# Local attention and two feed-forward layers on one core: loads merged, mask matmul cut into four tiles, order of the work re-timed

## The chip, the cores and the metric

The kernel runs on one core of a Trainium2 chip. The metric is the device time of one execution in microseconds (us). Three runs of the kernel before gave 480.46, 482.44 and 484.45 us, so the median is 482.44 us.

## The reference

Attention first, for 2 batches, 8 heads, 576 positions, 64 channels; then two feed-forward layers over 1152 tokens, 512 channels and 2048 hidden units. The weights are held as 64-bit words, q, k and v as 32-bit floats.

```python
# attention: mean over groups of 4 positions, dense; plus a band |i-j| < 4 at full length
out_d = sm_attn(q_d, k_d, v_d); out_up = np.repeat(out_d, 4, axis=2)
scores = np.where(np.abs(pos[:, None] - pos[None, :]) < 4, scale * q @ k.T, -1e9)
x = out_up + softmax(scores) @ v            # then [B*S, H*D]
h = x @ w_in                                # layer 1
P = a[0] + a[1]*h + a[2]*h**2 + a[3]*h**3
Q = 1 + abs(b[0])*abs(h) + abs(b[1])*h**2
x = (P / (Q + 1e-6)) @ w_out
h = x @ w_in2                               # layer 2
out = (h * np.tanh(softplus(h))) @ w_out2
```

## The kernel before, in words

**Attention** is cut into units (`unit`, L629). A unit is one pair of heads and four windows of 64 positions; a window is worked as two halves of 32 queries that each look at 48 keys. The ninth window of a batch, left over in each of the four pairs, makes a "mixed" unit that holds one window from each pair, so there are 16 plain units and 2 mixed ones. A pair of heads is made ready once per batch by `prep` (L548): it loads k (L554, L558), transposes it on TensorE (L546), scales it (L587), sums groups of four keys (L597), loads v for the dense part (`vload`, L605, two transfers of 64 and 8 rows) and sums it on POOL (L615, L619). A unit loads q (L639; four transfers where mixed), loads the values of its windows (L653; four transfers, or eight where mixed), transposes q, and in `pe_b` (L699) puts the mask into PSUM with one matmul (eye2 times mask, L702), adds 32 score matmuls of 48 columns (L709) and 8 or 32 dense ones of 144 columns (L717). Each of these works on a 64 by 32 tile of the array. Softmax runs on DVE, ACT and POOL; the transposes of the weights are L786 and L791; L816 and L826 multiply with the values. The result is split into two halves, xh and xl, for exact products.

**The layers** multiply 128-row blocks three times each (high by high, high by low, low by high): L1144 and L1277 in layer 1, L1458, L1514 and L1279 in layer 2, where L1458 belongs to a seven-product scheme whose sums L1480 adds on DVE (`plus`). **Weights** come in 32 tiles of 1 MB (L983, L988) into two raw buffers and are turned into floats: ACT L1000 and L1007, DVE L1014, then the high half (L1026) and the low half (L1031).

**The order** of all instructions on every engine is written out by a planner (`Plan.run`, L114). It plays the kernel through with a cost in us for each task (`add({"dve": 0.43}, ...)`) and issues, on each engine that is free, the ready task with the lowest priority number whose buffers are free. The program keeps that order: an instruction that waits holds everything behind it on its engine. All loads and stores are issued from SP. Priorities are due times: unit i of the first chunk has PROL + PSTEP*i + UOFF[i], its q load lies LOFF earlier, the k load KOFF earlier, the window values VOFF later, the dense values VROFF later; a weight tile is loaded LLEAD ahead and turned into floats CLEAD ahead of its use plus GOFF. The planner has a model of the transfers: at most QUEUED = 8 are under way, each with an issue time and a moving time (L221 to L226). When TensorE has nothing to do in the plan, it gets a **dummy**, a matmul of zeros (`warm`, L526, 480 columns).

Window values have NVW = 2 buffers, q has 3, raw weights 2. The mask is built at the start: two `affine_select` of POOL make `band` (L452, L455), and `masks` (L459) copies it on DVE, 12 copies in three tasks; `under` (L486) zeroes the lower half of eye2 and mask.

Of the kernel before, what the change touches and what calls it, by code (L numbers as in the profile page):

```python
# [12 lines left out]
BF16 = mybir.dt.bfloat16  # L13
# [4 lines left out]
ALU = mybir.AluOpType  # L18
AX = mybir.AxisListType

NEG = -1.0e9
# [58 lines left out]
class Plan:  # L80
# [33 lines left out]
    def run(self, names):  # L114
# [79 lines left out]
        while True:  # L194
            for e in names:
# [3 lines left out]
                while ready[e]:  # L199
# [73 lines left out]
def kernel(  # L273
# [22 lines left out]
    TW = 384  # L296
# [8 lines left out]


    ident = const.tile([128, 128], F32, name="ident")
    eye2 = const.tile([128, 128], BF16, name="eye2")
    mask = const.tile([128, 11, WK], BF16, name="mask")
    band = const.tile([64, 92], BF16, name="band")  # L310
    blank = const.tile([128, 480], BF16, name="blank")
# [53 lines left out]
    kn_s = lay("att", NKN, 768, parts=96)  # L365
    vr_s = lay("att", 1, 1024, (4, 4, D), parts=72)
    qn_s = lay("att", NQN, 256)
    vw_s = lay("att", NVW, 512, (4, 2, D), parts=64 + WK)
    s_s = lay("att", 2, 256, (4, 64))
    pd_s = lay("att", 2, SD)  # L370
# [78 lines left out]


    def bands():
        nc.gpsimd.affine_select(  # L452
            out=band, in_=band, compare_op=ALU.is_ge, fill=NEG, base=-8, pattern=[[1, 92]], channel_multiplier=-1,
        )
        nc.gpsimd.affine_select(  # L455
            out=band, in_=band, compare_op=ALU.is_ge, fill=NEG, base=14, pattern=[[-1, 92]], channel_multiplier=1,
        )
# [13 lines left out]

    def eyes():
        for h in range(2):
            nc.vector.tensor_copy(out=eye2[:64, 64 * h:64 * h + 64], in_=ident[:64, :64])
# [11 lines left out]
    def under():  # L486
        nc.vector.memset(eye2[64:], 0.0)
        nc.vector.memset(mask[64:], 0.0)

    t_m = add({"dve": 0.1}, lambda: nc.vector.memset(band, 0.0), -1900)  # L490
    t_un = add({"dve": 0.4}, under, -880)
    t_cd = add({"dve": 0.6}, zeros, -1000)
    t_bn = add({"pool": 0.5}, bands, -900, after=[t_m])
    t_mk = [
        add({"dve": 0.2 + 0.05 * len(ws)}, lambda x=(i, ws): [masks(x[0], *w) for w in x[1]], (-890, MKP, MKP)[i], after=[t_bn])
        for i, ws in enumerate((((0, 1), (1, 1), (2, 1), (3, 1)), ((4, 4),), ((8, 4),)))
    ]
    t_bias = add({"pool": 0.1}, biases, -20)
    t_i16 = add({"dve": 0.26}, eyes, -900, after=[t_id])
    t_ab = add({"sp": 0.9}, c_sp, -34, dma=[(0.65, 0.1), (0.5, 0.1)])  # L500
    A0, A1, A2, A3 = (cf[:, i:i + 1] for i in range(4))
    S0, S1 = (cf[:, i:i + 1] for i in range(4, 6))

# [26 lines left out]
    plan.filler = (warm_s + sc_s + pt_s + po_s, ((t_bl, warm),), 0.19)  # L530


    class Unit:
# [14 lines left out]
    def prep(bb, p, prio, slots, start):  # L548
# [62 lines left out]
        m0 = add({"sp": 1.25}, vload, prio + VROFF, take=[vr], chain="vr", dma=[(0.65, 0.8), (0.6, 0.12)])  # L611

        def va(e):
            tv = vr.v
# [14 lines left out]
    def unit(u, slots, start):  # L629
# [4 lines left out]
        qn, vw, qp, qT, qx = Buf(qn_s + xq), Buf(vw_s + xv), Buf(slots["q"]), Buf(qT_s), Buf(qx_s)  # L634
        sc, pt, po, px = Buf(slots["s"]), Buf(slots["pt"]), Buf(slots["po"]), Buf(px_s)
        tm, s, pd, pT, od, xt = Buf(tm_s), Buf(s_s), Buf(pd_s), Buf(pT_s), Buf(od_s), Buf(xt_s)
        mix = [qx] if mixed else []

        def qload():  # L639
            for i, p in enumerate(pairs):  # L640
                w, m = wins[i][1], n // len(pairs)
                src = q[bb, 2 * p:2 * p + 2, 64 * w:64 * w + 2 * m, :]
                nc.sync.dma_start(  # L643
                    out=qn.v[m * i:m * i + m].rearrange("p (r h d) -> p r h d", h=2, d=D),
                    in_=src.rearrange("h (p r) d -> p r h d", r=2),
                )

        l0 = add({"sp": 0.65}, qload, prio - LOFF, take=[qn], chain="ld", dma=[(0.65, 0.24)] * 4 if mixed else [(0.65, 0.58)])

        m0 = MASK0[kind]  # L650
        keys = [(p, [window(kind, w, b) for b in range(2)]) for p, w in wins]

        def vload():  # L653
            for w0, nb in ((0, 4), (2, 4)) if not mixed else [(w, 2) for w in range(4)]:
                p, (k0, k1) = keys[w0]
                for hh in range(2):
                    src = v[bb, 2 * p + hh]
                    nc.sync.dma_start(
                        out=vw.v[64 * (w0 // 2):64 * (w0 // 2) + WK, 2 * (w0 % 2):2 * (w0 % 2) + nb, hh, :],
                        in_=bass.AP(src.tensor, src.offset + k0 * D, [[D, WK], [(k1 - k0) * D, nb], [1, D]]),  # L660
                    )

        vl = add({"sp": 1.0}, vload, prio + VOFF, take=[vw], chain="vw", dma=[(0.45, 0.11)] * 8 if mixed else [(0.45, 0.33)] * 4)

        def pe_a():
            q2 = qp.v[:, :2 * n].rearrange("c (p r) -> c p r", r=2)
            for r in range(2):
                flip(q2[:, :, r], qn.v, r, n)
# [30 lines left out]
        def pe_b():  # L699

            hs = [slice(0, 64), slice(64, 128)]
            nc.tensor.matmul(  # L702
                sc.v[:, :nw * WK], eye2, mask[:, m0:m0 + nw].rearrange("p w x -> p (w x)"), start=True, stop=False,
            )
# [17 lines left out]
        tb = add(  # L722
            {"pe": 1.6 if mixed else 0.86}, pe_b, prio,
            after=tq + [kv_done[p] for p in pairs] + [t_i16, t_un, t_mk[kind]],
            take=[sc, tm, s, pd],
            use=[qT] + mix, chain="pb",
        )
# [81 lines left out]
        def pe_e():  # L809
# [10 lines left out]
            for m in range(2):  # L820
                for b in range(2):
                    for hh in range(2):
                        for a in range(2):
                            h, r = hs[hh ^ a], slice(64 * a, 64 * a + WK)
                            c = 128 * m + h.start + HB * b
                            nc.tensor.matmul(  # L826
                                px.v[h, a, 64 * m + HB * b:64 * m + HB * b + HB], vw.v[r, 2 * m + b, hh ^ a, :],
                                pT.v[r, c:c + HB], start=True, stop=True,
                            )

# [603 lines left out]
    def seven(st):  # L1434
# [42 lines left out]
        def plus(dst, i, src, after, and_=None):  # L1477
# [96 lines left out]
```

## Time and profile before

| what | us |
|---|---|
| median of three runs | 482.44 (480.46 to 484.45) |
| the profiled execution's own time | 482.31 |
| its span, first to last instruction | 480.4 |
| TensorE matmul busy | 469.4 (98%) |
| TensorE weight load busy | 429.1 (89%) |
| DVE busy | 377.0 (78%) |
| ACT busy | 338.3 (70%) |
| POOL busy | 57.1 (12%) |

Around the span lie 1.9 us. A busy time counts overlapping instructions once; matmuls follow one another before the former has ended, so the spacing of their starts, not their duration, is what one costs. The transfer lines count the 16 DMA engines of the core together.

### The profile page before, as it was taken

What the parts mean: (1) busy time and instruction counts of PE and PEld (TensorE: products, weight loads), DVE (VectorE), ACT (ScalarE), POOL (GpSimd) and SP (SyncE); (2) the same over time, 40 slices, a digit from 0 to 9 for tenths busy, and PEclk for the clock granted to TensorE, in tenths of its full rate; (3) what the DMA queues carried; (4) which work ended last, traced back from release to release, by engine and by line L of the source; (5) the groups of instructions that cost most, each with busy time, mean ns of one, the idle gap of its engine ahead of it and who ended that gap; (6) DMA issues with size and microseconds to landing.
All of it is one profiled execution on the core that took longest, in us unless ns stands there. A gap on an engine that the chain in (4) does not pass through costs nothing.

```text
span 480.4 us, 9823 instructions
## 1 busy us (share of the span) xinstructions
PE 469.4 (98%) x4052; PEld 429.1 (89%) x4052; DVE 377.0 (78%) x565; ACT 338.3 (70%) x529; POOL 57.1 (12%) x80
## 2 busy tenths in 40 slices
PE   8998999999999999999999999999999999999996
PEld 4667888889999999999999999898989898989885
DVE  6677999899899968997998999988596669524342
ACT  5678898786889799998879797578666446422320
POOL 2644434563000000000000000000000000000000
PEclk9999999999999999999999999999999999999999
DMA  9878887611522312343022022134304220000103
GB/s 170 196 178 198 243 200 188 166 37 35 176 89 88 123 54 89 96 125 131 0 89 88 1 88 89 39 111 146 143 15 162 87 89 1 1 0 0 67 0 132
DMA packets 45981, 47.18 MB, mean 98 GB/s; under 512 B 30576, under 2 KB 31344, under 8 KB 45936
## 3 DMA queue, kind: packets, MB, share of 16 engines
q1 hardware_dynamic: 45936, 46.54, 33.7%
q8 instruction: 32, 0.52, 0.5%
q14 instruction: 13, 0.11, 0.1%
HBM read 44.17 MB, written 2.36 MB: 97 GB/s over the span
## 4 chain that ended last, share of the span: by engine, by line
PE 73%; DVE 13%; DMA 8%; ACT 3%; SPq 2%; issue 1%; ACTq 0%
PE psum L1279 19%; PE psum L1144 18%; PE psum L1277 15%; PE psum L1458 11%; PE psum L1514 5%; DMA att<-in_q_dram 3%; DMA raw<-in_moe_w_in_dram 3%; DVE wt L1014 1%; PE psum L826 1%; DMA att<-in_v_dram 1%; DVE xl L1300 1%; PE psum L546 1%; SPq L643 1%; DVE wrk L1318 1%; DVE wo L1031 1%
## 5 line engine op out<-in xcount | busy, mean ns | idle before, releaser
L1144 PE MATMUL psum<-xh,wi 128*128 128x384 f32 (+1 forms) x336 | 83.4, 319 | 0.2 <-DVE wrk L1173 0.2
L1277 PE MATMUL psum<-gg,wo 128*128 128x384 f32 (+1 forms) x480 | 76.3, 313 | 0.0
L1277 PEld LDWEIGHTS psum<-gg,wo 128*128 128x128 f32 x480 | 72.8, 189 | 0.4 <-issue 0.2
L1144 PEld LDWEIGHTS psum<-xh,wi 128*128 128x128 f32 x336 | 59.1, 189 | 1.4 <-issue 0.9
L1144 PE MATMUL psum<-xl,wi 128*128 128x384 f32 (+1 forms) x168 | 52.4, 312 | 0.0
L1279 PE MATMUL psum<-wo,gg 128*128 128x512 f32 x216 | 51.7, 391 | 0.0
L1279 PE MATMUL psum<-wo,late_g 128*128 128x512 f32 x216 | 51.3, 391 | 0.0
L1279 PEld LDWEIGHTS psum<-wo,late_g 128*128 128x128 f32 x216 | 40.4, 188 | 8.0
L1279 PEld LDWEIGHTS psum<-wo,gg 128*128 128x128 f32 x216 | 40.4, 188 | 7.9
L1014 DVE SCALAR_TENSOR_TENSOR wt<-wt,raw 128x1024 int32<-128x1024 int32 x32 | 40.0, 1252 | 6.8 <-ACT wt L1000 6.5
L1000 ACT ACTIVATE wt<-raw 128x1024 f32<-128x1024 f32 x32 | 36.5, 1140 | 10.9 <-DVE wo L1031 4.8
L1007 ACT ACTIVATE raw<-raw 128x1024 int32<-128x1024 uint16 x32 | 36.7, 1147 | 5.1 <-DMA raw<-in_moe_w_out_dram 3.4
L1514 PE MATMUL psum<-xh,wi 128*128 128x384 f32 x128 | 34.5, 335 | 0.0
L1144 PEld LDWEIGHTS psum<-xl,wi 128*128 128x128 f32 x168 | 31.8, 189 | 0.0
L1390 DVE TENSOR_TENSOR part<-psum,part 128x512 f32<-128x512 f32 x27 | 17.8, 687 | 13.7 <-PE psum L1279 13.7
L1144 PE MATMUL psum<-xh,late_r 128*128 128x384 f32 x96 | 25.5, 334 | 0.0
L527 PE MATMUL psum<-blank 128*128 128x480 bf16 x86 | 22.9, 390 | 1.2 <-DVE band L490 1.2
L1031 DVE TENSOR_TENSOR wo<-wt,wo 128x1024 fp32r<-128x1024 f32 x14 | 17.1, 1219 | 8.7 <-ACT wo L1026 8.7
L1026 ACT ACTIVATE wo<-wt 128x1024 fp32r<-128x1024 f32 x11 | 11.7, 1062 | 17.1 <-DVE wt L1020 7.7
L1514 PEld LDWEIGHTS psum<-xh,wi 128*128 128x128 f32 x128 | 23.3, 188 | 0.2
L1164 ACT ACTIVATE wrk<-psum 128x768 f32<-128x768 f32 (+1 forms) x27 | 19.8, 734 | 5.1 <-PE psum L1144 4.8
L1088 ACT ACT_TABLE_LOAD x17 | 21.8, 1283 | 0.3
(165 smaller groups left out, 1043.5 us busy)
## 6 DMA issues: line engine op xcount, KB each, us to landing
raw<-in_moe_w_in_dram SPq DMA_DIRECT2D x16, 1024.0 KB, 6.0
raw<-in_moe_w_out_dram SPq DMA_DIRECT2D x16, 1024.0 KB
att<-in_v_dram SPq DMA_DIRECT2D x64, 48.0 KB, 4.0
out_dram<-part SPq DMA_DIRECT2D x9, 256.0 KB, 2.1
att<-in_q_dram SPq DMA_DIRECT2D x16, 128.0 KB, 4.2
att<-in_k_dram SPq DMA_DIRECT2D x6, 288.0 KB, 4.5
att<-in_v_dram SPq DMA_DIRECT2D x6, 256.0 KB, 5.7
wrk<-in_k_dram SPq DMA_DIRECT2D x2, 288.0 KB
```

The costliest lines, as they stand in the source:

```text
L527: nc.tensor.matmul(view[:, :480], blank[:, :128], blank, start=True, stop=True)
L1000: nc.scalar.activation(out=t.v, in_=words(r)[:, :, 1].bitcast(F32), func=AF.Prelu if fold else AF.Identity, scale=2.0 ** -112, **({"alpha" ...
L1007: nc.scalar.activation(out=words(r)[:, :, 0], in_=r.v.bitcast(U16).rearrange("p (n four) -> p n four", four=4)[:, :, 1], func=AF.Copy, sca ...
L1014: nc.vector.scalar_tensor_tensor(out=ti, in0=ti, scalar=3, in1=words(r)[:, :, 0], op0=ALU.logical_shift_left, op1=ALU.bitwise_or)
L1031: ENG[e].tensor_tensor(out=w.v[:, 1], in0=s.v, in1=w.v[:, 0].bitcast(F32), op=ALU.subtract)
L1088: nc.scalar.preload_act_table_set(name)
L1144: nc.tensor.matmul(st.h.v[:, i, :T], w.v[:, ww, ks], xx[:, kk, c0:c0 + T], start=(nn == 0 and (st.big or i == 0)), stop=(nn == 3 * KD - 1 ...
L1164: nc.scalar.activation(out=vw(st.a), in_=H(), func=AF.Square)
L1277: nc.tensor.matmul(A(d)[:, :T], w.v[:, ww, lo + d * 128:lo + (d + 1) * 128], vw(gg)[:, i, :], start=start, stop=stop)
L1279: nc.tensor.matmul(A(d), vw(gg)[:, i, sl], w.v[:, ww, lo:lo + DM], start=start, stop=stop)
L1458: nc.tensor.matmul(dst.v[:, :TW], wv.v[:, ww, at:at + 128], x(h, kk), start=bool(take) and nn == 0, stop=nn == 5, skip_group_check=not take,)
L1514: nc.tensor.matmul(h.v[:, i, :TW], w.v[:, ww, at:at + 128], xx[:, kk, c0:c0 + TW], start=nn == 0, stop=nn == 3 * KD - 1)
```

## The change

It does the following.

- Window values get a third buffer (NVW 3). A mixed unit's values come in four transfers in place of eight; the four windows lie in another order in the buffer.
- A mixed unit's q comes in one transfer in place of four, as 64 positions by 8 heads, and is transposed by four transposes of 64 rows. It takes the place of two of the q buffers.
- The dense values of a pair come in one transfer of 72 rows in place of two of 64 and 8 rows (8 pairs).
- The mask matmul of 128 rows by 128 columns becomes four on tiles of 64 by 32; eye2, mask and band are laid out twice, in the upper and the lower 64 partitions. `under` goes; `masks` makes 24 copies in place of 12, `bands` four `affine_select` in place of two.
- The two loads of a and b move from SP to ACT's queue and to the very start.
- Dummies have 416 columns in place of 480.
- The planner adds 0.8 us of moving time for every 7 us moved (FETCH, for packets that load instructions). The due times change: CLEAD 14 to 20, LLEAD 40 to 30, OLAG 18 to 26, KOFF 9 to 17, and others. `plus` (L1480) gets a priority 15 earlier.

```diff
-LEAD, CLEAD, LLEAD, OLAG = 38, 14, 40, 18
-PROL, PSTEP, VOFF, VROFF, LOFF, KOFF = -45, 2.5, 2, -1, 7, 9
+LEAD, CLEAD, LLEAD, OLAG = 38, 20, 30, 26
+PROL, PSTEP, VOFF, VROFF, LOFF, KOFF = -45, 3.0, -1, 3, 8, 17
-NKN, NVW, NXT, NQN = 2, 2, 3, 3
+NKN, NVW, NXT, NQN = 2, 3, 3, 3
+FETCH = (0.8, 7.0)
-UOFF = [-3.0, 0.0, 0.0, 3.0, 4.5, 3.0, 3.0, -1.5, 6.0, 0.0, 0.0, -4.5, -4.5, 4.5, 6.0, 4.5, -1.5, -1.5]
-GOFF = [0.0, 0.0, 0.0, 0.0, -4.0, -4.0, -10.0, -6.0, 2.0, -4.0, 10.0, 12.0]
+UOFF = [1.5, 6.0, 6.0, 10.5, 13.5, 16.5, 4.5, 21.0, 9.0, 6.0, -6.0, -3.0, 0.0, 7.5, -1.5, 9.0, -7.5, -12.0]
+GOFF = [0.0, 2.0, 0.0, 4.0, -4.0, -4.0, -8.0, -30.0, 28.0, 2.0, -2.0, 22.0]
...
-                            moved = max(moved, end + 0.3) + move
+                            first = max(moved, end + 0.3)
+                            moved = first + move + FETCH[0] * (int((first + move) / FETCH[1]) - int(first / FETCH[1]))
...
-        for b in range(2):
-            h = slice(HB * b, HB * b + HB)
+        for r0 in range(0, 128, HB):
+            b, h = r0 // HB % 2, slice(r0, r0 + HB)
...
-        nc.sync.dma_start(out=a_sb, in_=a.partition_broadcast(128))
-        nc.sync.dma_start(out=b_sb, in_=b.partition_broadcast(128))
+        nc.scalar.dma_start(out=a_sb, in_=a.partition_broadcast(128))
+        nc.scalar.dma_start(out=b_sb, in_=b.partition_broadcast(128))
...
-        nc.tensor.matmul(view[:, :480], blank[:, :128], blank, start=True, stop=True)
+        nc.tensor.matmul(view[:, :416], blank[:, :128], blank, start=True, stop=True)
...
-            for lo, hi in ((0, 64), (64, 72)):
-                nc.sync.dma_start(out=dst[lo:hi], in_=src[lo:hi])
+            nc.sync.dma_start(out=dst, in_=src)
...
+            if mixed:
+                nc.sync.dma_start(out=qn.v, in_=q[bb, :, 64 * w:64 * w + 64].rearrange("h s d -> s h d"))
...
-            for w0, nb in ((0, 4), (2, 4)) if not mixed else [(w, 2) for w in range(4)]:
-                p, (k0, k1) = keys[w0]
-                for hh in range(2):
+            for a in range(2):
+                p, ks = keys[2 * a]
+                for i in range(2):
+                    src = v[bb, 2 * p + (0 if mixed else i)]
+                    k0, far = (ks[i], S) if mixed else (ks[0], ks[1] - ks[0])
...
-            nc.tensor.matmul(
-                sc.v[:, :nw * WK], eye2, mask[:, m0:m0 + nw].rearrange("p w x -> p (w x)"), start=True, stop=False,
-            )
+            for b in range(2):
+                for h in hs:
+                    r0 = h.start + HB * b
+                    nc.tensor.matmul(
+                        sc.v[r0:r0 + HB, :nw * WK], eye2[h, HB * b:HB * b + HB],
+                        mask[h, m0:m0 + nw].rearrange("p w x -> p (w x)"), start=True, stop=False, tile_position=(h.start, r0),
+                    )
...
-            return add({"dve": t_dve(TW)}, fn, pr, after=after, use=[src, dst])
+            return add({"dve": t_dve(TW)}, fn, pr - HP, after=after, use=[src, dst])
```

## Rows read from the trace of the kernel before

**Rows 1.** Busy time of the engines in five stretches (window, its length, engines, clock, DMA).
```profile
0.00:33.00 33.00, 30.01 (x488) 18.46 (x489) 21.81 (x72) 21.22 (x56) 15.98 (x30) 1.00 0.90 194
33.00:48.00 15.00, 13.38 (x276) 11.20 (x278) 11.07 (x34) 12.92 (x32) 6.14 (x10) 1.00 0.71 167
48.00:96.00 48.00, 46.68 (x838) 41.17 (x837) 45.11 (x91) 40.68 (x96) 22.80 (x26) 1.00 0.80 200
96.00:122.50 26.50, 25.95 (x538) 23.33 (x537) 24.52 (x51) 18.33 (x48) 11.66 (x16) 1.00 0.23 53
122.50:475.50 353.00, 352.36 (x1925) 334.36 (x1924) 272.71 (x318) 245.12 (x300) 0.52 (x1) 1.00 0.22 75
```

**Rows 2.** The same stretches, the dummies of L527 alone (PE, PEld, clock, DMA).
```profile
0.00:33.00 33.00, 17.39 (x67) 6.82 (x67) 1.00 0.90 194
33.00:48.00 15.00, 1.07 (x4) 0.29 (x3) 1.00 0.71 167
48.00:96.00 48.00, 4.04 (x15) 1.42 (x15) 1.00 0.80 200
```

**Rows 3.** The chain that ended last, up to 60 us (start, us, what).
```profile
17.15 2.02 SPq L983
19.27 6.06 DMA att<-in_q_dram
...
26.64 6.37 DMA raw<-in_moe_w_in_dram
...
35.94 0.66 SPq L643
36.65 0.61 SPq L643
37.31 0.61 SPq L643
37.96 5.14 DMA att<-in_q_dram
43.10 0.09 issue
43.19 0.41 PE psum L546 x2
```

**Rows 4.** PE timeline: mask matmul, a unit's scores, dummies, first L1144.
```profile
21.62 0.25 PE L702 MATMUL psum<-mask,eye 128*128 128x192 bf16 x1
21.80 0.55 PE L709 MATMUL psum<-att 64*32 64x48 f32 x32
...
29.39 1.78 PE L527 MATMUL psum<-blank 128*128 128x480 bf16 x8
...
32.74 0.38 PE L527 MATMUL psum<-blank 128*128 128x480 bf16 x1
32.78 0.46 PE L1144 MATMUL psum<-xh,wi 128*128 128x256 f32 x1
```

**Rows 5.** The chain again: two transposes of 128 columns, a mixed unit's 32 dense matmuls.
```profile
44.31 0.22 PE psum L786 x2
...
48.43 0.98 PE psum L717 x32
```

**Rows 6.** DMA queue of the first 33 us (packets, MB, share of 16 engines).
```profile
q1 hardware_dynamic: 10508, 6.32, 88.7%
```

**Rows 7.** What SP waited for up to 120 us, then from 92 to 120 us.
```profile
SPq L658 <- PE psum L826: 12.6, 6, 4.7
...
SPq L658 <- PE psum L826: 11.2, 4, 4.7
```

**Rows 8.** SP's timeline: loads of a and b; issues of dense values at the start.
```profile
2.62 1.19 SPq L609 DMA_DIRECT2D att<-in_v_dram  x2
...
27.37 0.49 SPq L481 DMA_DIRECT2D a_sb<-in_moe_a_dram  x1
27.90 0.43 SPq L482 DMA_DIRECT2D b_sb<-in_moe_b_dram  x1
```

**Rows 9.** DVE at the start: mask copies, then the first sum over q.
```profile
2.81 2.35 DVE L464 COPY mask<-band 32x48 bf16<-32x48 bf16 x12
...
6.36 0.42 DVE L683 TENSOR_REDUCE att<-psum 128x64 f32<-128x256 f32 x1 [1.20 <-PE psum L546]
```

**Rows 10.** Waits over the span: ACT for raw weights, PE for window values, for L1480.
```profile
ACT wt L1000 <- DMA raw<-in_moe_w_in_dram: 4.2, 4, 2.3
...
308.25 0.44 PE L1458 MATMUL psum<-xh,late_r 128*128 128x384 f32 x1 [0.64 <-DVE wrk L1480]
```

**Rows 11.** Landing times of the w_in loads (issue to landing, min/median/max).
```profile
DMA to landing us min/median/max: 5.0/6.0/9.4
```

More of the change, by code (lines that the diff above doesn't have):

```diff
@@ L307 @@
     ident = const.tile([128, 128], F32, name="ident")
-    eye2 = const.tile([128, 128], BF16, name="eye2")
+    eye2 = const.tile([128, 64], BF16, name="eye2")
     mask = const.tile([128, 11, WK], BF16, name="mask")
-    band = const.tile([64, 92], BF16, name="band")
-    blank = const.tile([128, 480], BF16, name="blank")
+    band = const.tile([128, 92], BF16, name="band")
+    blank = const.tile([128, 416], BF16, name="blank")
     a_sb = const.tile([128, 4], F32, name="a_sb")
@@ L367 @@
     qn_s = lay("att", NQN, 256)
+    qm_s = [Place("att", qn_s[-2].lo, 512, (8, D), 64)]
     vw_s = lay("att", NVW, 512, (4, 2, D), parts=64 + WK)
@@ L451, in bands @@
     def bands():
-        nc.gpsimd.affine_select(
-            out=band, in_=band, compare_op=ALU.is_ge, fill=NEG, base=-8, pattern=[[1, 92]], channel_multiplier=-1,
-        )
-        nc.gpsimd.affine_select(
-            out=band, in_=band, compare_op=ALU.is_ge, fill=NEG, base=14, pattern=[[-1, 92]], channel_multiplier=1,
-        )
+        for h in (slice(0, 64), slice(64, 128)):
+            nc.gpsimd.affine_select(
+                out=band[h], in_=band[h], compare_op=ALU.is_ge, fill=NEG, base=-8, pattern=[[1, 92]], channel_multiplier=-1,
+            )
+            nc.gpsimd.affine_select(
+                out=band[h], in_=band[h], compare_op=ALU.is_ge, fill=NEG, base=14, pattern=[[-1, 92]], channel_multiplier=1,
+            )
     def masks(kind, w, n):
-        for b in range(2):
-            h = slice(HB * b, HB * b + HB)
+        for r0 in range(0, 128, HB):
+            b, h = r0 // HB % 2, slice(r0, r0 + HB)
             lo = window(kind, w, b) - 64 * w + 11
@@ L473, in eyes @@
         for h in range(2):
-            nc.vector.tensor_copy(out=eye2[:64, 64 * h:64 * h + 64], in_=ident[:64, :64])
+            nc.vector.tensor_copy(out=eye2[64 * h:64 * h + 64], in_=ident[64 * h:64 * h + 64, 64 * h:64 * h + 64])
     def biases():
@@ L480, in c_sp @@
     def c_sp():
-        nc.sync.dma_start(out=a_sb, in_=a.partition_broadcast(128))
-        nc.sync.dma_start(out=b_sb, in_=b.partition_broadcast(128))
+        nc.scalar.dma_start(out=a_sb, in_=a.partition_broadcast(128))
+        nc.scalar.dma_start(out=b_sb, in_=b.partition_broadcast(128))
     add({"act": 1.3}, lambda: nc.scalar.preload_act_table_set("natural_log_exp_and_others"), -1000)
     t_id = add({"pool": 1.1}, lambda: make_identity(nc, ident), -1000)
-    def under():
-        nc.vector.memset(eye2[64:], 0.0)
-        nc.vector.memset(mask[64:], 0.0)
     t_m = add({"dve": 0.1}, lambda: nc.vector.memset(band, 0.0), -1900)
-    t_un = add({"dve": 0.4}, under, -880)
     t_cd = add({"dve": 0.6}, zeros, -1000)
-    t_bn = add({"pool": 0.5}, bands, -900, after=[t_m])
+    t_bn = add({"pool": 1.0}, bands, -900, after=[t_m])
     t_mk = [
-        add({"dve": 0.2 + 0.05 * len(ws)}, lambda x=(i, ws): [masks(x[0], *w) for w in x[1]], (-890, MKP, MKP)[i], after=[t_bn])
+        add({"dve": 0.4 + 0.1 * len(ws)}, lambda x=(i, ws): [masks(x[0], *w) for w in x[1]], (-890, MKP, MKP)[i], after=[t_bn])
         for i, ws in enumerate((((0, 1), (1, 1), (2, 1), (3, 1)), ((4, 4),), ((8, 4),)))
@@ L499 @@
     t_i16 = add({"dve": 0.26}, eyes, -900, after=[t_id])
-    t_ab = add({"sp": 0.9}, c_sp, -34, dma=[(0.65, 0.1), (0.5, 0.1)])
+    t_ab = add({"act": 1.15}, c_sp, -2000, dma=[(0.65, 0.1), (0.5, 0.1)])
     A0, A1, A2, A3 = (cf[:, i:i + 1] for i in range(4))
@@ L607, in vload @@
             dst = vr.v.rearrange("p (h t) f d -> p h (t f d)", h=2)
-            for lo, hi in ((0, 64), (64, 72)):
-                nc.sync.dma_start(out=dst[lo:hi], in_=src[lo:hi])
-        m0 = add({"sp": 1.25}, vload, prio + VROFF, take=[vr], chain="vr", dma=[(0.65, 0.8), (0.6, 0.12)])
+            nc.sync.dma_start(out=dst, in_=src)
+        m0 = add({"sp": 0.65}, vload, prio + VROFF, take=[vr], chain="vr", dma=[(0.65, 1.0)])
         def va(e):
@@ L633, in unit @@
         xq, xv = (wide_s["qn"], wide_s["vw"]) if start else ([], [])
-        qn, vw, qp, qT, qx = Buf(qn_s + xq), Buf(vw_s + xv), Buf(slots["q"]), Buf(qT_s), Buf(qx_s)
+        qn, vw, qp, qT, qx = Buf(qm_s if mixed else qn_s + xq), Buf(vw_s + xv), Buf(slots["q"]), Buf(qT_s), Buf(qx_s)
         sc, pt, po, px = Buf(slots["s"]), Buf(slots["pt"]), Buf(slots["po"]), Buf(px_s)
@@ L639, in qload @@
         def qload():
-            for i, p in enumerate(pairs):
-                w, m = wins[i][1], n // len(pairs)
-                src = q[bb, 2 * p:2 * p + 2, 64 * w:64 * w + 2 * m, :]
+            w = wins[0][1]
+            if mixed:
+                nc.sync.dma_start(out=qn.v, in_=q[bb, :, 64 * w:64 * w + 64].rearrange("h s d -> s h d"))
+            else:
                 nc.sync.dma_start(
-                    out=qn.v[m * i:m * i + m].rearrange("p (r h d) -> p r h d", h=2, d=D),
-                    in_=src.rearrange("h (p r) d -> p r h d", r=2),
+                    out=qn.v.rearrange("p (r h d) -> p r h d", h=2, d=D),
+                    in_=q[bb, 2 * pairs[0]:2 * pairs[0] + 2, 64 * w:64 * w + 2 * n].rearrange("h (p r) d -> p r h d", r=2),
                 )
-        l0 = add({"sp": 0.65}, qload, prio - LOFF, take=[qn], chain="ld", dma=[(0.65, 0.24)] * 4 if mixed else [(0.65, 0.58)])
+        l0 = add({"sp": 0.65}, qload, prio - LOFF, take=[qn], chain="ld", dma=[(0.45 if mixed else 0.65, 0.58)])
         m0 = MASK0[kind]
@@ L653, in vload @@
         def vload():
-            for w0, nb in ((0, 4), (2, 4)) if not mixed else [(w, 2) for w in range(4)]:
-                p, (k0, k1) = keys[w0]
-                for hh in range(2):
-                    src = v[bb, 2 * p + hh]
+            for a in range(2):
[3 more added lines that the diff above has]
+                    k0, far = (ks[i], S) if mixed else (ks[0], ks[1] - ks[0])
+                    here = vw.v[64 * a:64 * a + WK]
                     nc.sync.dma_start(
-                        out=vw.v[64 * (w0 // 2):64 * (w0 // 2) + WK, 2 * (w0 % 2):2 * (w0 % 2) + nb, hh, :],
-                        in_=bass.AP(src.tensor, src.offset + k0 * D, [[D, WK], [(k1 - k0) * D, nb], [1, D]]),
+                        out=here[:, 2 * i:2 * i + 2].rearrange("k w h d -> k (w h) d") if mixed else here[:, :, i],
+                        in_=bass.AP(src.tensor, src.offset + k0 * D, [[D, WK], [far * D, 4], [1, D]]),
                     )
-        vl = add({"sp": 1.0}, vload, prio + VOFF, take=[vw], chain="vw", dma=[(0.45, 0.11)] * 8 if mixed else [(0.45, 0.33)] * 4)
+        vl = add({"sp": 1.0}, vload, prio + VOFF, take=[vw], chain="vw", dma=[(0.45, 0.33)] * 4)
         def pe_a():
+            if mixed:
+                for i in range(nw):
+                    nc.tensor.transpose(
+                        qp.v[:, 64 * i:64 * i + 64], qn.v[:, 2 * i:2 * i + 2].rearrange("s h d -> s (h d)"), ident[:64, :64],
+                    )
+                return
             q2 = qp.v[:, :2 * n].rearrange("c (p r) -> c p r", r=2)
@@ L722, in unit @@
         tb = add(
-            {"pe": 1.6 if mixed else 0.86}, pe_b, prio,
-            after=tq + [kv_done[p] for p in pairs] + [t_i16, t_un, t_mk[kind]],
+            {"pe": 1.52 if mixed else 0.78}, pe_b, prio,
+            after=tq + [kv_done[p] for p in pairs] + [t_i16, t_mk[kind]],
             take=[sc, tm, s, pd],
@@ L826, in pe_e @@
                             nc.tensor.matmul(
-                                px.v[h, a, 64 * m + HB * b:64 * m + HB * b + HB], vw.v[r, 2 * m + b, hh ^ a, :],
+                                px.v[h, a, 64 * m + HB * b:64 * m + HB * b + HB], vw.v[r, 2 * b + m if mixed else 2 * m + b, hh ^ a, :],
                                 pT.v[r, c:c + HB], start=True, stop=True,
```

4 lines of the change are left out of this document (2 added, 2 removed).

## The prediction

> **What bounds the kernel now.** I read the busy times by stretch first. From 122.5 to 475.5 us TensorE is busy for 352.36 of 353 us, at a granted clock of 1.00 (2.4 GHz) [rows 1]: this part is matmul work that the change doesn't touch, and it can't shrink. What can shrink is time in which TensorE waits, and that lies ahead of 122.5 us in two forms: idle time, and dummies. Dummies show as busy, so the second view counts them [rows 2]. Eight of them in a row take 1.78 us with the last one's tail of 0.38, so one costs (1.78 - 0.38) / 7 = 0.20 us [rows 4], and the loss is:
>
> - 0 to 33 us: 67 x 0.20 = 13.4 us of dummies and 33 - 30.01 = 3.0 us idle, 16.4 us;
> - 33 to 48: 4 x 0.20 + 1.6 = 2.4 us;
> - 48 to 96: 15 x 0.20 + 1.3 = 4.3 us;
> - 96 to 122.5: 0.55 us, with no dummy; after that 0.64 us at one place [rows 10].
>
> So 24.3 us are lost in all and every gain comes out of these. The cut at 33 us is where the first hidden-layer matmul starts, 32.78 us [rows 4]. The third view, the chain that ended last, says what the waits are: up to 48 us it runs through SP's issues and the landings of q and of the first weights, 5 to 6.4 us each [rows 3]. The DMA engines are 0.90 busy up to 33 us, 0.71 in the next stretch, 0.80 up to 96 us and 0.23 after it [rows 1]. The early part is bound by transfers and their order, the late part by TensorE.
>
> **The change part by part.** The sum goes against the profiled execution, 482.31 us, which is within 0.15 us of the median, so the same figure serves for both.
>
> *Mixed q in one transfer.* On the chain, three issues of 0.66, 0.61 and 0.61 us precede the last of the four q transfers, whose landing takes 5.14 us and lets TensorE go on at 43.2 us [rows 3]. One issue in their place takes 1.9 us out of the chain. The loss of that stretch is 2.4 us, so all of it can be had: -1.9 us. The bytes stay the same. If the k load and the values behind it come later instead, the gain is 0; if the q moves ahead of the weight load before it as well, it is the whole 2.4. The second mixed unit's q and values come at the end of attention, where TensorE has no dummies: nothing there.
>
> *Dense values in one transfer, a and b from ACT.* Two issues take 1.19 us [rows 8], so four pairs up to 33 us free 4 x 0.6 = 2.4 us of SP, and a and b free 0.49 + 0.43 = 0.9 us. But the queue's own share is 88.7% of 33 us [rows 6], so only 3.7 us of the stretch are free for transfers to move into, and the first landing takes its part of these. Of the 3.3 us I count 1.3. The loads of a and b then stand ahead of the table load on ACT, which has nothing else to do up to the first landing; cost nothing. If the cover is gone, 0.9 us.
>
> *Due times in the first 33 us.* 6.32 MB move there [rows 6]; the first chunk needs 4 pairs and 4 units: by the shapes 4 x (0.29 k + 0.13 q + 0.29 v + 0.19 window values) + one weight tile of 1.05 MB = 4.7 MB. The other 1.6 MB, at 194 GB/s 8.2 us, come early for what follows. Loading k 8 us earlier and weights 10 us later in due time can bring the needed part forward, but what is put off is due directly afterwards. I take -1.5 us, from 0 to -8.2; with the issues that is -2.8 us of 16.4.
>
> *Third buffer for window values, four transfers for eight.* SP waits 12.6 us for L826 to give such a buffer back, which looks like the prize. But 11.2 us of these lie from 92 us on [rows 7], where TensorE is busy for 25.95 of 26.5 us [rows 1]. Only 1.4 us stand in the hungry part. The mixed unit saves four issues as well. From 48 to 96 us, where 4.3 us are lost, I take a third, -1.4 us; the ends are 0 and -4.3. After 96 us -0.3 us.
>
> *Mask in four tiles.* Now the mask matmul starts 0.18 us before the first score matmul [rows 4]. A tile needs 192 columns, by the dummies' 0.20 us for 480 columns 0.08 us. Four at once make 0.08, one after the other 0.32 us. The trace has the same tiles: a mixed unit's 32 dense matmuls of 144 columns take 0.98 us, while two f32 transposes of 128 columns take 0.22 us [rows 5]. So a matmul of 144 columns alone would need 0.12 us and 32 of them 4.0 us: four run at once. I take 0.08, 18 x -0.10 = -1.8 us of TensorE work. Where TensorE waits for loads this only makes room for a dummy: half the units stand past 48 us, -0.9 us. The ends are -1.8 and 18 x 0.14 = +2.5 us.
> The Trainium skill speaks against this: its page "TensorEngine Tiling (Array Packing)", section "Restrictions and Gotchas", says that different row tiles can't use one PSUM bank at the same time. All four mask tiles write one bank from two row halves, so two rounds would be needed, 0.16 us, and the gain would be 18 x -0.02 = -0.4 us. The trace's dense matmuls write one bank from both row halves and don't bear this out.
>
> *Mask copies.* 12 copies take 2.35 us on DVE up to 5.16 us, and then DVE stands 1.2 us until q has been transposed [rows 9]. Twelve more, at 0.196 us, end some 2.0 us later (the memsets that go give back 0.4), so the first sum over q comes 0.8 us late; k's sums stand behind it. The first landing sets that stretch, and dummies follow; I count +0.4, ends 0 and +0.8.
>
> *Dummies of 416 columns.* A dummy ends 0.03 us earlier where real work becomes ready in its course; with some 20 groups of dummies and half of that each -0.3 us, ends 0 and -0.6. If the shorter ones lost the granted 1.00, each us at 1.2 GHz would cost half a us; no stretch ahead of 475.5 us shows that [rows 1].
>
> *`plus` earlier.* The 0.64 us [rows 10] go if DVE gets to L1480 in time: -0.5 us, ends 0 and -0.64, since what is passed is not needed sooner. The chance that a later DVE step then waits is left in the range.
>
> Sum: -1.9 - 2.8 - 1.4 - 0.3 - 0.9 + 0.4 - 0.3 - 0.5 = -7.7 us. These are not independent: the first three want the same free DMA time, and DVE is 45.1 of 48 us busy from 48 us and 24.5 of 26.5 us after it [rows 1], so what TensorE does earlier must find DVE earlier, too. I strike a fifth: -6.2 us, **476.1 us**. The likeliest case's own range is 473 to 479 us.
>
> **The rivals.**
>
> *Transfers were hidden anyway.* The queue is full up to 33 us, what is loaded earlier displaces something else, and the third buffer works where TensorE is busy. For it: 0.90 busy DMA, and rows 7. Against it: 0.71 in the next stretch. Then the mixed q's half, the mask and `plus` stay: -1.0 - 0.9 - 0.5 + 0.4 = -2.0, 480.3 us.
>
> *The weights come late (slower).* The planned time from a weight load to its turning falls from 40 - 14 = 26 to 30 - 20 = 10 us of due time. A w_in load takes 5.0 to 9.4 us to land [rows 11]. The point from which this decides is a landing 10 us after the load's due time: then L1000 waits on ACT, and the softmax steps queued behind it, and DVE behind these. Now ACT loses 4.2 us in 4 such waits, 1.05 each [rows 10]. Eight tiles are loaded up to 96 us; if every one waited as long, and half of the gain stayed, 482.3 + 8 x 1.05 - 3.1 = 487.6 us. Against it: half of the landings take 6.0 us or less, and none 10.
>
> *Dense values on fewer DMA engines.* 72 rows don't divide by sixteen; if they go to twelve engines with six rows each, that is more than the five rows of the busiest engine now, where 64 and 8 rows are spread. By the stretch's mean, 33 x 0.887 / 6.32 = 4.6 us a MB [rows 6], 0.288 MB take 1.33 us spread evenly at 4.5 rows; five rows are 1.48 us, six 1.78. Four such loads up to 33 us and four after it, 0.3 us each, cost 2.4 us if nothing else fills the free engines: 478.5 us.
> The Trainium skill has the rule of this case on "DMA: Bandwidth & Descriptors", section "Why a DMA increments its semaphore by 16 and not by 1": a transfer uses the largest number of engines up to 16 that divides its slowest dimension, for 72 that is 12. The trace's rows add up all engines, so no row shows it yet.
>
> *More than I count.* With the order right, the put-off 8.2 us and the 4.3 us become reachable to a good half: about -11 us, 471 us.
>
> **How the numbers follow.** Forecast 0.46, more than that 0.13, transfers hidden 0.20, fewer engines 0.10, weights late 0.11. A measurement of this kernel tells about 1% from no change, 4.8 us: faster is below 477.6, slower above 487.3 (the three runs differ by 4). The forecast is below 477.6 in four fifths of its cases, 0.37, the greater gain always, fewer engines in a third, 0.03, hidden in 0.02: 0.55. Weights late is above 487.3 in somewhat over half, and a tail from broken order elsewhere brings it to 0.09. The rest, 0.36, is same. The range goes from 470 (greater gain) to 483 (hidden, with the mask's dear end), leaving out the late weights.
>
> **What would show it.** Right: fewer than 67 dummies up to the first L1144 and that start before 31 us; no idle time of some 1.6 us behind the first mixed q, and one q issue there; L702's four tiles 0.08 to 0.1 us ahead of L709; SP's wait for L826 gone without a change of TensorE after 96 us; the dense stretch of layer 2 as long as before. Wrong: dummies as many as before (hidden), ACT waits for raw weights of over 2 us in number (late), landings of the dense values longer than now (fewer engines).

## The result and the profile after

The changed kernel takes 484.63 us (median of 17 runs, 483.48 to 487.61) where the kernel before took 481.62 in as many runs on the same chips. The ratio is 1.006 (95% interval 1.0044 to 1.0076): slower by 0.6%, where 476.1 us and a gain of over 1% were forecast. The profiled execution took 484.25 us, its span 482.5. A few executions in this document ran in a slower state of the chip; they count in the medians and not in the ratios.

The same five stretches of the changed kernel, all engines (to be read against [rows 1]):

```profile
0.00:33.00 33.00, 30.00 (x477) 19.26 (x478) 22.09 (x86) 19.96 (x57) 14.45 (x31) 1.00 0.90 196
33.00:48.00 15.00, 15.00 (x282) 11.69 (x281) 10.84 (x24) 11.59 (x26) 7.94 (x10) 1.00 0.55 138
48.00:96.00 48.00, 48.00 (x841) 41.85 (x840) 45.32 (x90) 40.53 (x93) 21.79 (x23) 1.00 0.76 198
96.00:122.50 26.50, 26.50 (x577) 24.00 (x577) 25.97 (x56) 19.73 (x54) 13.96 (x18) 1.00 0.21 49
122.50:475.50 353.00, 352.31 (x1983) 334.57 (x1982) 273.98 (x321) 246.06 (x302) 0.78 (x1) 1.00 0.23 77
```

And its dummies alone (L526 now; against [rows 2]):

```profile
0.00:33.00 33.00, 18.66 (x83) 8.27 (x83) 1.00 0.90 196
33.00:48.00 15.00, 5.80 (x28) 2.40 (x27) 1.00 0.55 138
48.00:96.00 48.00, 6.12 (x28) 2.49 (x28) 1.00 0.76 198
```

From 33 to 122.5 us TensorE is never idle, and it does less for it: 56 dummies stand there where 19 stood, 139 in all against 86. Ten in a row (at 20.20 us) take 1.92 us with the last one's tail of 0.34, so one costs (1.92 - 0.34) / 9 = 0.175 us. The loss, counted as in the prediction, is 83 x 0.175 + 3.0 = 17.5 us up to 33 us (16.4 before), 4.9 us up to 48 (2.4), 4.9 up to 96 (4.3), none up to 122.5 (0.55), and 0.7 after it: 28.0 us against 24.3. If the 18 mask matmuls each give back the 0.09 us shown below, that is 1.6 us, and 3.7 - 1.6 = 2.1 us is the difference of the spans. The sum is rough, since the tail of the matmul ahead of a gap counts as busy, and the 1.6 us were not shown by themselves. But it says what has to be explained: where the waits, now dummies, come from.

The chain that ended last, by engine, before and after:

```profile
PE 73%; DVE 13%; DMA 8%; ACT 3%; SPq 2%; issue 1%; ACTq 0%
```

```profile
PE 85%; DVE 11%; ACT 3%; issue 1%; ACTq 0%
```

Transfers and SP's issues made 10% of it and are gone. In their place stands TensorE's own order, the dummies in it.

The loads don't all come earlier. The third w_in tile is issued at 32.82 us for 35.49, but the first mixed q at 46.60 us for 35.94. The first w_in tile is issued when it was before (17.14 us) and must have landed by about 24.5 us, as no w_in load takes longer than 6.9 us; yet ACT, whose order now has the softmax of two units ahead of it, turns it into floats 5 us later. ACT before, then ACT and the first hidden-layer matmul of the changed kernel:

```profile
24.36 1.12 ACT L1000 ACTIVATE wt<-raw 128x1024 f32<-128x1024 f32 x1 [0.44 <-DMA raw<-in_moe_w_in_dram]
```

```profile
29.37 1.14 ACT L1011 ACTIVATE wt<-raw 128x1024 f32<-128x1024 f32 x1
...
36.21 0.43 PE L1155 MATMUL psum<-xh,wi 128*128 128x256 f32 x1
```

That matmul started at 32.78 us before [rows 4]. What SP waited for in the changed kernel, for a buffer of window values (L659) and for the first mixed q (L640):

```profile
SPq L659 <- PE psum L837: 12.4, 10, 3.0
...
SPq L640 <- PE psum L545: 3.3, 1, 3.3
```

The first is as long as before, 12.6 us [rows 7], with three buffers in place of two. The second is new: the mixed q lies over two of the plain q buffers, and SP holds back all that stands behind it until the transposes (L545) have read these.

Two places of the start, first TensorE and then DVE of the changed kernel (against [rows 4, 9]); the column after the time is the duration:

```profile
9.43 0.55 PE L720 MATMUL psum<-att 64*32 64x48 f32 x32 [0.89 <-ACT att L682]
...
13.11 0.26 PE L712 MATMUL psum<-mask,eye 64*32 64x192 bf16 x4
13.20 0.51 PE L720 MATMUL psum<-att 64*32 64x48 f32 x32
```

```profile
6.02 1.32 DVE L468 COPY mask<-band 32x192 bf16<-32x192 bf16 x6
7.37 0.16 DVE L513 TENSOR_REDUCE cf<-cf 128x1 f32<-128x4 f32 x1
...
8.40 0.23 DVE L505 TENSOR_SCALAR cf<-a_sb,cf 128x3 f32<-128x3 f32 x1
8.54 0.42 DVE L690 TENSOR_REDUCE att<-psum 128x64 f32<-128x256 f32 x1
```

At 13.11 us the four tiles stand 0.09 us ahead of the scores (0.18 before), and all four take 0.26 us, as long as the one matmul of before with its tail: they run at once. On DVE (the first line has the last six of the 24 mask copies) the first sum over q starts at 8.54 us, 6.36 before. The copies end at 7.34 us, 2.2 us later than before, and the arithmetic on a and b, which had come at 34 us before, takes the next 1.2 us. The first unit's scores start at 9.43 us, where the kernel before had them at 8.25.

The mixed q (L640) is one transfer now, and TensorE goes on to its transposes (L669) without a gap:

```profile
46.60 0.63 SPq L640 DMA_DIRECT2D att<-in_q_dram  x1
```

```profile
51.47 0.46 PE L669 MATMUL psum<-ident,att 64*128 64x64 f32 x4
```

### The profile page after: what moved, and what is told of

Same layout as the page of the kernel before. It is cut to its first block, busy times and chain, and to the rows that moved or that the text cites. A ratio compares the mean times of both kernels' runs of the same rounds, so it can differ in the third digit from the quotient of the medians.

```text
span 482.5 us, 10023 instructions
## 1 busy us (share of the span) xinstructions
PE 474.9 (98%) x4163; PEld 433.6 (90%) x4163; DVE 380.3 (79%) x576; ACT 337.9 (70%) x528; POOL 58.9 (12%) x82
## 4 chain that ended last, share of the span: by engine, by line
PE 85%; DVE 11%; ACT 3%; issue 1%; ACTq 0%
PE psum L1155 20%; PE psum L1290 18%; PE psum L1288 16%; PE psum L1469 11%; PE psum L1525 5%; PE psum L526 4%; PE psum L837 2%; PE psum L827 2%; PE psum L545 1%; PE psum L720 1%; PE psum L728 1%; PE psum L797 1%; DVE mask L468 1%; PE psum L802 1%; DVE xl L1311 1%
## 5 line engine op out<-in xcount | busy, mean ns | idle before, releaser
L526 PE MATMUL psum<-blank 128*128 128x416 bf16 x139 | 30.9, 355 | 1.1 <-DVE band L490 1.1
L1535 ACT ACTIVATE wrk<-psum 128x768 f32<-128x768 f32 x7 | 5.7, 814 | 24.5 <-PE psum L1525 24.5
L526 PEld LDWEIGHTS <-blank 128*128 128x128 bf16 x139 | 13.3, 101 | 10.5 <-issue 2.6
```

The source lines that it names most:

```text
L526: nc.tensor.matmul(view[:, :416], blank[:, :128], blank, start=True, stop=True)
```

## The experiments

Ratios are to the kernel before, run on the same chip, with the 95% interval. The first question was whether the dummies are the loss or only its mark.

**Dummies left out.** In both kernels the order stays as planned, and a dummy past 20 us of the planned time isn't written out:

```diff
-                    fns[-1](s.view)
+                    if now < 20:
+                        fns[-1](s.view)
```

> The changed kernel with the same order, but its 81 dummies past 20 us of the planned time left out (58 of 139 stay). Theory 1, the dummies stand in TensorE's order where the plan expected late transfers, and on the chip the data is there: without them TensorE goes on at once, 81 x 0.173 = 14 us of dummies go and idle time comes back for a part; at most 480 us, over 4 us below the changed kernel. Theory 2, the dummies only fill waits for loads and softmax: idle time takes their place and the time stays at 483 to 486 us. Theory 3, the clock needs them: the granted clock falls below 1.00 in the stretch 24 to 60 us and the time rises above 486 us.

> The kernel before with the same order, its 44 dummies past 20 us of the planned time left out (42 of 86 stay). Theory 1: here TensorE also had 6.9 us of idle time, so fewer of its dummies were in the way; 1 to 3 us less than before. Theory 2: no change, 481 to 483 us. Theory 3: the granted clock falls and the time rises.

Measured: 484.91 us for the changed kernel, ratio 1.0082 (1.0051 to 1.0114); 481.14 for the one before, 0.9999 (0.9967 to 1.0031). Nothing is gained in either. The stretch from 24 to 36 us says why for the changed one (window, length, PE, PEld, DVE, ACT, POOL, clock, DMA):

```profile
24.00:36.00 12.00, 9.15 (x185) 6.24 (x174) 7.81 (x22) 8.61 (x24) 9.04 (x12) 0.72 0.88 235
```

The granted clock is 0.72 there, a mean of the two levels, with TensorE busy for 9.15 of 12 us; in the kernel before without these dummies it is 0.72 in the same stretch, too. The first hidden-layer matmul of the changed one does start earlier, 34.31 us for 36.21. By the trace, 58 x 0.175 us of dummies and 10.9 us of idle time are 21.1 us lost, where the full set had 28.0; yet the span is only half a microsecond shorter (482.0). The rest fell to the clock, which stands at 0.50 for 10.2 us in all, and to the tails ahead of new gaps. Theories 1 and 3 act against each other, so half of the dummies came next:

```diff
+        count = [0]
...
-                    fns[-1](s.view)
+                    count[0] += now >= 20
+                    if now < 20 or count[0] % 2:
+                        fns[-1](s.view)
```

> The changed kernel in its own order, with every second dummy past 20 us of the planned time left out (99 of 139 stay). With all 81 of them left out TensorE got ahead but its clock fell to 0.72 in the stretch from 24 to 36 us and nothing was gained. Theory 1 with theory 3 (the dummies stand in the way, and some of them are needed for the clock): with half of them the clock stays near 1.00 and 1 to 4 us of the 40 x 0.173 = 7 us go, 481 to 484 us. Theory 2 (they only fill waits): 484 to 486 us, idle time in their place.

Measured: 482.33 us, ratio 1.0040 (1.002 to 1.0059). The clock holds at 1.00:

```profile
24.00:36.00 12.00, 10.45 (x224) 6.71 (x212) 8.17 (x22) 8.44 (x24) 9.03 (x12) 1.00 0.85 234
36.00:48.00 12.00, 10.79 (x247) 9.11 (x243) 9.65 (x20) 11.05 (x24) 6.41 (x8) 1.00 0.54 123
```

The full set had TensorE busy for 11.25 and 12.00 us in these two windows: a part of the 40 dummies left out came back as idle time. The time by itself, 482.33 us, lies where theories 1 and 3 had it, but this chip runs the kernel before in 480.80: by the ratios 0.2% is gained, about 1 us of 7, and the intervals of 1.0040 and 1.0060 overlap. Most of the dummies mark a wait that the order has anyway.

**The start on DVE.** The order stays; the 12 copies for the lower 64 partitions go and one memset takes their place.

```diff
+    m_first = [1]
...
-        for r0 in range(0, 128, HB):
+        if m_first:
+            m_first.clear()
+            nc.vector.memset(mask[64:], 0.0)
+        for r0 in range(0, 64, HB):
```

> The changed kernel in its own order, with the 12 mask copies of the lower 64 partitions left out and one memset to zero in their place, so that one head of each pair has no mask and the output differs. DVE has about 2.0 us less to do up to 7.3 us. Theory 4, the start on DVE sets the first unit and is carried to the end: scores of the first unit at about 8.2 in place of 9.43 us, and 1 to 1.5 us less than the changed kernel in all, some 483.3 us. Rival: the second unit waits for loads or for dummies in the order anyway, and the total moves by less than 0.5 us.

Measured: 483.54 us, ratio 1.0062 (1.0038 to 1.0087). The scores of the first unit start at 8.12 us, as forecast, 1.3 us earlier. The ratio is that of the changed kernel (1.006), and the profiled span was 480.5, 2 us shorter. The two don't agree, and how much of the late start reaches the end stays open; it isn't what costs the 0.6%.

**The edits alone, in the order of before.** The planner keeps its old costs, so the order of the instructions stays as it was, and only the code of a task changes.

> The kernel before in its own order, with the mask in four tiles alone: 24 copies, four selects on POOL, no zeroing of the lower halves. If the tiles save 0.08 us a unit as the trace of the changed kernel shows (0.09 us ahead of the scores in place of 0.18) and the start costs 1.2 us, the two nearly cancel: -0.9 + 1.2, 481.5 to 482.5 where the kernel before has 481.6. If the start is covered by the first loads: 480.5. If tiles cost somewhere else: above 483.

```diff
...
-            nc.tensor.matmul(
-                sc.v[:, :nw * WK], eye2, mask[:, m0:m0 + nw].rearrange("p w x -> p (w x)"), start=True, stop=False,
-            )
+            for b in range(2):
+                for h in hs:
+                    r0 = h.start + HB * b
+                    nc.tensor.matmul(
+                        sc.v[r0:r0 + HB, :nw * WK], eye2[h, HB * b:HB * b + HB],
+                        mask[h, m0:m0 + nw].rearrange("p w x -> p (w x)"), start=True, stop=False, tile_position=(h.start, r0),
+                    )
```

Measured: 480.42 us, ratio 0.9986 (0.9962 to 1.001): at most 0.4% either way, with the middle at -0.7 us.

> The kernel before in its own order, with the dense values of each pair in one transfer and a mixed unit's values in four, so 16 issues fewer on SP and nothing else. If SP's issues or the eight transfers under way held the loads back: 1 to 2 us faster than before, 479.6 to 480.6. If transfers were hidden: within 0.5 us. If the 72 rows on fewer DMA engines cost (0.3 us each), up to 2 us slower and longer landings of the dense values than 5.5 us.

```diff
-            for lo, hi in ((0, 64), (64, 72)):
-                nc.sync.dma_start(out=dst[lo:hi], in_=src[lo:hi])
+            nc.sync.dma_start(out=dst, in_=src)
...
-            for w0, nb in ((0, 4), (2, 4)) if not mixed else [(w, 2) for w in range(4)]:
+            for a in range(2):
...
```

Measured: 479.74 us, ratio 0.9973 (0.9947 to 0.9998): 1.3 us faster, barely clear of none, and what was expected if SP's issues held the loads back. If the 72 rows ran on fewer DMA engines, it cost nothing that shows.

> The kernel before in its own order, with a third place for window values used in turn, so that a load waits for the unit three back, not two; nothing else. The wait of SP for L826 falls from 12.6 to under 4 us. If the third buffer is worth what the prediction said (the wait lies where TensorE is busy): within 0.7 us of before. If it opens the loads earlier: 1.4 to 4 us faster.

```diff
+            real.append(vw_p[len(vw_n) % 3].view)
+            vw_n.append(1)
...
```

Measured: 480.51 us, ratio 0.9993 (0.9967 to 1.0019): no difference. SP's wait (L662 for L830 here) fell from 12.6 to 7.1 us, less than forecast:

```profile
SPq L662 <- PE psum L830: 7.1, 4, 2.5
```

> The kernel before in its own order, with the mask tiles, the merged value loads and a mixed unit's q in one transfer (into a place of its own); due times, transfer model and dummies as before. If these edits are worth what was forecast on the chain and only the new order loses it: about -0.7 (tiles, measured) - 1.3 (merged values, measured) - 1.9 (q, from the chain) = 477 us, at most 479; ratio to before 0.992 to 0.996. If q was covered by the next wait: 479 to 480. Theory that the edits themselves cost: above 481.

```diff
...
+    qm = lay("att", 1, 512, (8, D), parts=64)[0]
...
+                nc.sync.dma_start(out=qm.view, in_=q[bb, :, 64 * w:64 * w + 64].rearrange("h s d -> s h d"))
...
```

Measured: 477.5 us (12 runs, 476.2 to 483.36), ratio 0.9932 (0.9906 to 0.9957): 3.3 us faster by the ratio, and faster than both kernels. Its early stretches:

```profile
33.00:48.00 15.00, 15.00 (x344) 12.35 (x344) 12.63 (x36) 12.61 (x32) 5.69 (x9) 0.95 1.01 188
48.00:96.00 48.00, 48.00 (x889) 42.61 (x889) 46.26 (x98) 44.28 (x105) 26.12 (x29) 0.95 0.76 193
```

TensorE is as full as in the changed kernel, with 344 and 889 matmuls in these windows, 18 of them dummies, where that has 282 and 841 with 56 dummies. The clock column shows 0.95 for this one execution (477.09 us); others of the same kernel, at 0.998 and above, took 476.2 to 480.31 us, so the gain is not a matter of the clock. SP has no wait for the mixed q here, which has a place of its own. The run leaves out the third buffer, the shorter dummies, a and b from ACT and the earlier `plus`.

> All of the edits above, the third place, too, in the order of before, and every second dummy past 20 us of the planned time left out (64 of 86 stay). If edits and dummies add up: 1 us below the run with the edits alone, 476 to 478 us, faster than both kernels. If the clock falls or waits take the dummies' place: no faster than the run with the edits alone.

This adds the diffs of the third place and of half the dummies to the one above. Measured: 477.57 us, ratio 0.9926 (0.9899 to 0.9953): the same as without the third place and with all dummies. This pair is the best version found.

**The order.** With that, the new order must cost what the edits earn and more: 1.006 / 0.9932 = 1.013, some 6 us, with the few edits that the run above leaves out. Two replanned versions had been run beside the first ones.

> The changed kernel without the 0.8 us for every 7 us moved in the planner's model of transfers; all else, due times too, as changed. Theory 1: the plan expects less waiting, 129 dummies in place of 139, so some 2 us less than the changed kernel, 482 to 483. Theory 2: the model only reorders, and the time moves by under 1 us or rises because the due times were set for the other model.

```diff
-FETCH = (0.8, 7.0)
+FETCH = (0.0, 7.0)
```

Measured: 488.94 us (four executions), ratio 1.0123 (1.0028 to 1.0217): no faster than the changed kernel, though the order has 129 dummies in place of 139.

> The changed kernel's loads, mask tiles, third buffer, short dummies and early plus, with all due times of the kernel before and no 0.8 us: 107 dummies in the order. If the due times are what costs (theory 1 in its wide form), this lies below the kernel before, 478 to 481. If the new loads or the mask tiles themselves cost, it is slower than before, above 483.

```diff
-LEAD, CLEAD, LLEAD, OLAG = 38, 20, 30, 26
-PROL, PSTEP, VOFF, VROFF, LOFF, KOFF = -45, 3.0, -1, 3, 8, 17
+LEAD, CLEAD, LLEAD, OLAG = 38, 14, 40, 18
+PROL, PSTEP, VOFF, VROFF, LOFF, KOFF = -45, 2.5, 2, -1, 7, 9
```

FETCH, UOFF and GOFF go back to the values of before with them; NVW stays at 3. Measured: 482.77 us, ratio 1.003 (0.9999 to 1.006). With the same due times and nearly the same edits, in an order planned anew, that is 1.003 / 0.9932 = 1.010, 1% over the run with the old order. So it isn't the due times alone. But the mixed q over two q buffers is in this run, too, and SP waits 5.4 us for it; no run tells this from the new order. The last four runs ask, in the kernel before, what due times and small shifts cost.

> The kernel before with the due times of the changed one and nothing else (no third buffer, no 0.8 us, old loads, old mask): 117 dummies in the order in place of 86. Theory 5, the new due times cost: 486 to 490 us, the 7 us and what the edits had given back. Theory 6, any replanning costs: above 483, but no worse than the small shifts. If the due times only suit the new edits: above 490.

> The kernel before with one due time shifted by 1.5 us (the first unit, UOFF -3.0 to -1.5): 87 dummies for 86. Theory 5: within 1 us of before. Theory 6: the order shifts in many places, and the time is 1 to 8 us off before.

> The kernel before with PSTEP 2.6 in place of 2.5, so that five units of the first chunk are due up to 0.4 us later: 102 dummies for 86. Theory 5: within 1 us of before. Theory 6: 1 to 8 us slower, the more as the plan holds 16 more dummies.

> The kernel before with 1.2 in place of 1.1 us for the landing of a transfer in the planner's model, due times as they were: 118 dummies for 86. Theory 5: within 1 us of before. Theory 6: 1 to 8 us slower; with 32 more dummies of 0.20 us, 6 us if all stood in the way.

The first of these takes over the due times of the change and nothing else. The three small shifts:

```diff
-UOFF = [-3.0, 0.0, 0.0, 3.0, 4.5, 3.0, 3.0, -1.5, 6.0, 0.0, 0.0, -4.5, -4.5, 4.5, 6.0, 4.5, -1.5, -1.5]
+UOFF = [-1.5, 0.0, 0.0, 3.0, 4.5, 3.0, 3.0, -1.5, 6.0, 0.0, 0.0, -4.5, -4.5, 4.5, 6.0, 4.5, -1.5, -1.5]
```

```diff
-PROL, PSTEP, VOFF, VROFF, LOFF, KOFF = -45, 2.5, 2, -1, 7, 9
+PROL, PSTEP, VOFF, VROFF, LOFF, KOFF = -45, 2.6, 2, -1, 7, 9
```

```diff
-LAT = {"pe": 0.2, "act": 0.16, "dve": 0.15, "pool": 0.15, "sp": 1.1}
+LAT = {"pe": 0.2, "act": 0.16, "dve": 0.15, "pool": 0.15, "sp": 1.2}
```

Measured (4 to 10 executions each), with the dummies in the order:

| kernel | dummies | us | ratio |
|---|---|---|---|
| before | 86 | 480.91 | 1 |
| one unit due 1.5 us later | 87 | 481.15 | 0.9992 (0.9965 to 1.0018) |
| PSTEP 2.6 | 102 | 484.02 | 1.0071 (1.0037 to 1.0105) |
| landing 1.2 us in the model | 118 | 488.06 | 1.0139 (1.0114 to 1.0164) |
| new due times alone | 117 | 492.06 | 1.0218 (1.0178 to 1.0258) |

A tenth of a microsecond in one constant costs 0.7 or 1.4%, though no transfer, no buffer and no matmul but the dummies has changed. That is theory 6, in two shifts of three. The new due times alone cost more than either, 2.2%, so theory 5 holds beside it for the old loads. The shift that left the order's dummies at 87 cost nothing; the two that raised them to 102 and 118 cost 3.4 and 6.7 us by the ratios, where 16 and 32 dummies of 0.20 us are 3.2 and 6.4 us. This fits, and is not shown to be the cause: in the trace of PSTEP 2.6 TensorE idles for 4.4 us where it idled for 7.1 before, so a part of the new dummies took the place of idle time. Nor does the count give the size: 117 dummies cost more than 118.

## Why the prediction was wrong

*Where TensorE loses time* was read rightly: all of the difference lies ahead of 122.5 us (352.31 us busy in the dense part, 352.36 before).

*The edits* were sized rightly as a sum. Mixed q, merged loads, mask tiles and copies were put at -1.9 - 1.3 - 0.9 + 0.4 = -3.7 us; together, in the order of before and with a and b still on SP, they measured -3.3 us. The merged values alone gave 1.3 us, where 1.3 stood for the issues of dense values, a and b; the mixed unit's values, merged in the same run, were booked under the third buffer. The tiles with their copies gave about 0.7 us, not told from none; 0.5 was forecast. By difference some 1.3 us are left for the mixed q, put at 1.9. The tiles' time ahead of the scores, 0.09 us, came out as worked out from the dense matmuls (0.08). The Trainium skill's rule on row tiles and one PSUM bank ("TensorEngine Tiling (Array Packing)", "Restrictions and Gotchas") is not borne out by the trace here, where the two halves write different partitions of the bank: four tiles of two row halves took 0.26 us, as long as one.

*Mask copies* were put at +0.8 us for the first sum over q, with the loads as cover. The sum came 2.2 us late: about 1.0 us by the copies, and 1.2 us by the arithmetic on a and b, which now stands ahead of it and which the prediction, having their loads "cost nothing", didn't see. How much of that reaches the end was not settled.

*The third buffer*: the -1.4 and -0.3 us that were taken for it and for the four issues saved with it were too much. The buffer alone measured 0.07%, no difference from none, and in the changed kernel SP waits for one of three buffers as long as it did for one of two.

*`plus` earlier* was put at -0.5 us and gave nothing: TensorE waits 0.7 us for its sum (L1491) where it waited 0.64. *The shorter dummies*, -0.3 us, were not run alone.

*The step that failed* is the sentence on the due times in the first 33 us: "I take -1.5 us, from 0 to -8.2". The new order was given a gain and two ends on one side. The other terms, too, were taken against an order that the trace of before shows, as if it stayed. But none of that order is kept: every constant changes it from the start to the end of attention. In its place the runs showed that a new order, by due times or by another constant, costs between nothing and 2.2% (the new due times alone, in the kernel before), and none was faster. Here the fall from -3.3 us to +2.9 us, 1.3% or about 6 us, is that term, with what the mixed q over two q buffers and the other edits not run alone may add. The prediction has "a tail from broken order elsewhere" in its chance for slower, but no price for it.

*The rivals.* "Weights come late" named the other side, but by another mechanism. The w_in loads land sooner than before [rows 11], and no wait of ACT for a raw w_in tile is left in the early part:

```profile
DMA to landing us min/median/max: 5.2/5.5/6.9
```

The first weights still reach TensorE 3.4 us later than before, but through the order of ACT, which takes them up 5 us after they landed.

"Transfers hidden anyway" is wrong for the edits: in the old order the merged loads do pay. "Fewer engines" shows no cost in time; no view tells on how many engines the 72 rows ran.

*The signs given in advance.* The one on dummies held, but for the wrong rival: 83 of them for 67 up to 33 us was to mean "hidden". It meant that the order now waits by its own writing, while the queue is as full as before (0.90) and the transfers have left the chain. The first hidden-layer matmul was to start before 31 us and started at 36.21. SP's wait for L826 was to go and stayed (12.4 us). The single q issue with no gap behind it, the 0.09 us of the tiles and the dense stretch came as said.

What stays open: which of the new due times cost most, and whether the old order is good because it had been picked by time on the chip, or by luck. No run replans with the true costs of the mask copies (the plan has 1.8 us for the 24 that take 4.8) and of the transfers.

## What to carry to other kernels

Where a planner writes the order, an edit has two prices: its own, and that of the new order. Measure them apart, by keeping the old order while only the code of a task changes. A profile of before can price the first; for the second it gives no bound on the dear side. Here replanning cost 0 to 2.2%, against the order of the kernel before. And fillers written into an in-order queue are the plan's forecast of waiting: count them in the order, before and after. Every order here with over 100 of them, for 86, was slower than its edits alone would make it, but the count didn't rank these.

## What the hardware showed that was not expected

With 81 dummies left out, TensorE was busy for 9.15 of 12 us from 24 to 36 us, nearly all of it attention matmuls, and the granted clock was still 0.72; with half of them back, it was busy for 10.45 us and the clock 1.00. Half of the dummies were enough to hold the clock there. But the busy share of a window doesn't settle it: from 12 to 24 us the merged loads in the old order, with all dummies, show 10.30 us and 0.86, the best version 10.22 us and 1.00.

A mean granted clock of 0.95 cost nothing that shows. In the run of the edits with that clock, dummies started every 0.211 us for 0.203 before, so TensorE was slower; but the dense matmuls of 512 columns of layer 2 started every 0.227 us in both.
